# Sorting V as rows through DRAM in a Sinkhorn attention and feed-forward kernel

## The chip, the cores and the metric

The kernel runs on one core of a Trainium2 chip. The metric is the device time in microseconds (us) of one execution. The engines are TensorE (PE; its weight loads are shown as PEld), VectorE (DVE), ScalarE (ACT), GpSimd (POOL) and SyncE (SP). SP and POOL also issue DMAs; each has its own queue, and an engine takes its instructions in the order in which they are written.

## The reference

Four batches of eight heads, 768 positions, 64 elements a head. The 768 positions are cut into 8 blocks of 96. A small matrix P (8 x 8 for each batch and head) is made from `sort_net` by five rounds of softmax and column normalisation, and mixes the blocks of K and of V; attention then runs inside each block, and a feed-forward network with a squared ReLU follows.

```python
for _ in range(5):
    P = exp(P - P.max(-1)); P = P / (P.sum(-1) + 1e-9); P = P / (P.sum(-2) + 1e-9)
k_sorted = einsum('bhij,bhjcd->bhicd', P, k_b)      # the same for v
scores = scale * q_b @ k_sorted.T                   # block by block
attn = softmax(scores);  y = attn @ v_sorted
x = y as rows of 8 * 64 = 512                       # 3072 tokens
out = (s * relu(x @ w_in)**2 + b) @ w_out           # 512 -> 2048 -> 512
```

## The kernel before

The 3072 tokens are worked in eight tiles of 384 (two per batch: `half` 0 and 1, each of four blocks). For each tile `ffn1` multiplies by `w_in` (tiles `hps`, 128 matmuls of 384 columns), ACT takes the ReLU into `rt` and DVE squares it into `gt`; `ffn2` multiplies by `w_out` (tiles `ops`, three row groups of 16 matmuls of 512 columns), DVE adds scale and bias into `ot`, and SP stores it.

The order of the work is written out by hand. PE runs ffn1 of both tiles of a batch b, then ffn2 of both. `ffn2` takes a dictionary of slots: after each group of four `ops` matmuls the pieces in that slot are issued, and so the attention of the next batch n = b + 1 is laid into the two ffn2 of batch b. Slots 0 to 11 belong to one ffn2. In the first ffn2, slot 2 holds the three pieces of K sorting, slots 5 and 9 the four pieces of V sorting, slot 9 the first two score pieces, and slot 11 the first product with V:

```python
s0 = {2: [K(n, 0, "A"), K(n, 1, "D"), K(n, 2, "A")],
      5: [V(n, 0, "D"), V(n, 1, "A"), V(n, 2, "D")],
      9: [V(n, 3, "D"), SC(n, 0, 0), SC(n, 0, 1)],
      11: [P(n, 0, 0), SC(n, 0, 2), SC(n, 0, 3)]}
```

How K and V are sorted: `k_piece` (L252) takes 16 positions of K at a time. The 128 partitions hold head, block and half-block (`h j z`), and a matrix `PD[b]` made of P and masks (`build_pd`, from `jsel`, `bm`, `PT`, `RC`) picks and mixes. `v_piece` (L302) does the same for V with the roles of the operands changed: the data are the weights (128 x 64), so the result has the position on the partition, as `p_piece` needs it. For this V is first permuted from (c d) to (d c) into `VP`: for batch 0 by ACT during the start-up, for batches 1 to 3 by POOL in eight copies (`v_sort`, L171). A V piece is 32 matmuls of 64 columns and an evacuation of 1024 elements a partition from PSUM into `VS`; there are four pieces a batch. `VS` holds 48 positions on partitions 0 to 47 and 48 more on 64 to 111, with a column pair of ones (the softmax sum) behind each block's 64 values and zeros between; `fill_vs` writes these.

`s_piece` (tiles `sc`) makes the scores and ACT their exponentials `at`; `p_piece` (tiles `pv`, L352) multiplies by `VS`, and DVE divides into `x`. Queries are loaded as `qtok`, one DMA per block, and turned into `qt` by two DMA transposes on SP (`q_dma`, L294), which stand ahead of the first ffn2 of batch b; `x` is turned into `xt` by DMA transposes (`t_dma`, L389).

Loads for batch 1 are issued by POOL after the weights (`loads(1)`: K, V, eight of Q, then the eight permutes). Loads for batches 2 and 3 stand behind a small copy, `gate`, which waits for the first `gt` of a later ffn1. PSUM tiles come from two pools: `psa` (three buffers of two banks: `hps`, K, V, scores, pv) and `psb` (two of one bank: `ops` among others). `ot` has three buffers.

Of the kernel before, what the change touches and what calls it, by code (L numbers as in the profile page):

```python
# [9 lines left out]
FP = mybir.dt.float32  # L10
# [6 lines left out]
def spread(t, dims):  # L17

    return bass.AP(tensor=t.tensor, offset=t.offset, ap=[list(t.ap[0])] + dims)
# [3 lines left out]
def kernel(  # L23
# [32 lines left out]

    raw = [t.rearrange("b h (j z c) d -> b (h j z) (c d)", j=NB, z=2) for t in (q, k, v)]

    const = ctx.enter_context(tc.tile_pool(name="const", bufs=1))
    rawp = ctx.enter_context(tc.tile_pool(name="rawp", bufs=2))  # L60
    trp = ctx.enter_context(tc.tile_pool(name="trp", bufs=2))
# [5 lines left out]
    osb = ctx.enter_context(tc.tile_pool(name="osb", bufs=3))  # L67
    psa = ctx.enter_context(tc.tile_pool(name="psa", bufs=3, space=bass.MemoryType.PSUM))
    psb = ctx.enter_context(tc.tile_pool(name="psb", bufs=2, space=bass.MemoryType.PSUM))
    ctx.enter_context(tc.manual_schedule())  # L70


# [11 lines left out]
    def load(t, b, parts=1):  # L84
        ti = rawp.tile([128, C2, D], BF, tag=f"raw{t}", name=f"raw{t}")
        RAW[t, b] = ti
        n = C2 // parts
        for c in range(0, C2, n):
            nc.gpsimd.dma_start(out=ti[:, c:c + n, :].rearrange("p c d -> p (c d)"),
                                in_=raw["qkv".index(t)][b][:, c * D:(c + n) * D])  # L90

    QTOK = {}

    def load_q(b, ns=range(NB)):
# [4 lines left out]
        for n in ns:  # L99
# [2 lines left out]
    zeros = const.tile([128, 512], BF)  # L102
    nc.vector.memset(zeros[:, 0:128], 0.0)  # L103
    nc.vector.memset(zeros[:, 128:512], 0.0)  # L104
    VP = [const.tile([128, D, GAP], BF, name=f"vp{i}") for i in range(2)]
    KS = [const.tile([128, NG, 2, GAP], BF, name=f"ks{i}") for i in range(2)]
    VS = [const.tile([KR, 2 * NG, VW], BF, name=f"vs{i}") for i in range(2)]
    nc.vector.memset(VP[0][:, :, C2:GAP], 0.0)
    nc.vector.memset(KS[0][:, :, :, C2:GAP], 0.0)
    nc.vector.memset(sne[:, NB, :], 1e-9)  # L110

# [3 lines left out]
    idv = ident.rearrange("p (a e j z) -> p a e j z", a=NHP, e=2, j=NB)  # L115
    emat = const.tile([BH, B, 128], FP)
    nc.gpsimd.memset(emat, 0.0)
    nc.gpsimd.affine_select(out=emat, in_=emat, pattern=[[-H, B], [-1, H], [0, 2 * NB]], base=0,
                            channel_multiplier=1, compare_op=ALU.not_equal, fill=1.0)
    load("k", 0, 3)  # L120
    load_q(0, range(HB))
# [27 lines left out]
    def fill_vs(i):  # L149
        nc.gpsimd.memset(VS[i][:, :, D:VW], 1.0)  # L150
        nc.gpsimd.memset(VS[i][32:GAP, :, D:VW], 0.0)
        nc.gpsimd.memset(VS[i][32:C2, :, D:VW], 1.0)

    fill_vs(0)
    Z = []

    def warm(n, w=512):
# [4 lines left out]
                             start=True, stop=True)  # L162


    def permute(eng, b, src, cs=slice(0, C2), ds=slice(0, D)):
        o = VP[b % 2][:, ds, cs]
        i = src[:, cs, ds].rearrange("p c d -> p d c")
        if eng is nc.scalar:
            eng.copy(out=o, in_=i)
        else:  # L170
            eng.tensor_copy(out=o, in_=i)  # L171


    rstat = const.tile([BH, NB], FP)
    rrec = const.tile([BH, NB], FP)
    jsel = const.tile([128, NB], FP)
    bm = const.tile([128, 2 * 2 * NHP], FP)
    idle = [
        lambda: nc.vector.tensor_reduce(
            out=jsel, in_=ident.rearrange("p (h j z) -> p j h z", h=H, j=NB), axis=AX.XY, op=ALU.add),  # L180
# [8 lines left out]
    for it in range(5):  # L189
        nc.scalar.activation(out=sn, in_=sn, func=AF.Exp)  # L190
        if it >= 1:
            permute(nc.scalar, 0, v0f, slice((it - 1) * CV, it * CV))
# [26 lines left out]
    def take_p(b0, n, pe):  # L219

        bs = slice(b0, b0 + n)
        tmp = rtp.tile([128, n * NB, NB], FP, tag=f"tmp{n}", name="tmp")
        nc.vector.tensor_tensor(out=tmp, in0=pe.rearrange("p b i j -> p (b i) j"),
                                in1=spread(jsel, [[0, n * NB], list(jsel.ap[1])]), op=ALU.mult)
        nc.vector.tensor_reduce(out=PT[:, bs].rearrange("p b i -> p (b i)"), in_=tmp, axis=AX.X,
                                op=ALU.add)
        cs = rtp.tile([128, n], FP, tag=f"cs{n}", name="cs")
        nc.vector.tensor_reduce(out=cs, in_=PT[:, bs], axis=AX.X, op=ALU.add)
        nc.vector.reciprocal(out=RC[:, bs], in_=cs)

    def build_pd(b):
        pd = const.tile([128, 2, 2, NG], BF, name=f"pd{b}")
        nc.vector.scalar_tensor_tensor(
            out=pd.rearrange("p e z (a i) -> p (e z a) i", i=NB),
            in0=spread(bm, [list(bm.ap[1]), [0, NB]]), scalar=RC[:, b:b + 1],
            in1=spread(PT[:, b], [[0, 4 * NHP], list(PT.ap[2])]), op0=ALU.mult, op1=ALU.mult)
        PD[b] = pd
# [53 lines left out]
    def q_dma(b):  # L291
        qt = q_tile(b)
        for n0 in (0, HB):
            nc.sync.dma_start_transpose(  # L294
                out=qt[:, n0:n0 + HB].rearrange("p n a t -> p (n a) t"),
                in_=QTOK[b][:, n0:n0 + HB].rearrange("p n h d -> p (n h d)"))

    def v_piece(b, d0, eng):
        ps = psa.tile([128, CK, 2 * NG], FP, tag="a", name="tv")
        for d in range(CK):  # L300
            for z in range(2):
                nc.tensor.matmul(out=ps[z * GAP:(z + 1) * GAP, d, :],  # L302
                                 lhsT=VP[b % 2][:, d0 + d, :], rhs=PD[b][:, :, z, :],
                                 start=True, stop=True)
        evac(eng, VS[b % 2][:, :, d0:d0 + CK], ps[0:KR].rearrange("p d g -> p g d"))

# [150 lines left out]
        nc.sync.dma_start(out=out[r0:r0 + 128, ns], in_=ot[:, ns])  # L457


    take_p(0, 1, spread_p(0, 1))  # L460
    build_pd(0)

    nc.gpsimd.tensor_copy(out=ones[:, 0:1], in_=PD[0][:, 0, 0, 0:1])
# [31 lines left out]
    nc.gpsimd.memset(sel, 0.0)  # L495
    for r in range(0, 128, 32):
        nc.gpsimd.memset(sel[r:r + 1], 1.0)
    nc.gpsimd.memset(VP[1][:, :, C2:GAP], 0.0)
    nc.gpsimd.memset(KS[1][:, :, :, C2:GAP], 0.0)
    fill_vs(1)  # L500
    for t, src in ((s_bc, moe_s), (b_bc, moe_b)):
        nc.gpsimd.dma_start(out=t, in_=src.to_broadcast([128, 1]))

    def v_sort(b):
        for i in range(8):
            permute(nc.gpsimd, b, RAW["v", b], ds=slice(i * 8, (i + 1) * 8))

    def loads(b):
        load("k", b)
        load("v", b)  # L510
        load_q(b)
        v_sort(b)

    loads(1)

# [22 lines left out]
    def V(b, i, eng): return lambda: v_piece(b, i * CK, eng)  # L538
# [12 lines left out]
    ffn1(1, {-2: [TP(0, 1, 2, "D")], 1: [lambda: take_p(1, B - 1, PB), PDB(1)], 4: [PDB(2)],  # L551
             5: [PDB(3), sum_w], 7: [make_bias]}, ahead=3)
    gate = const.tile([128, 1], BF)

# [7 lines left out]
    for b in range(B):  # L562
        n = b + 1
        if b:
            ffn1(2 * b, {0: [gated_loads(n)]} if n < B else {})
            ffn1(2 * b + 1, {})
        if n == B:
            ffn2(2 * b, {})
            ffn2(2 * b + 1, {})
            break  # L570
        q_dma(n)
        s0 = {
            2: [K(n, 0, "A"), K(n, 1, "D"), K(n, 2, "A")],
            5: [V(n, 0, "D"), V(n, 1, "A"), V(n, 2, "D")],
            9: [V(n, 3, "D"), SC(n, 0, 0), SC(n, 0, 1)],
            11: [P(n, 0, 0), SC(n, 0, 2), SC(n, 0, 3)]}
# [35 lines left out]
```

## Time and profile before

| | us |
|---|---|
| median of 3 runs | 228.69 (228.53 to 228.84) |
| the profiled execution | 228.41 |
| its span, from first to last instruction | 226.6 |
| PE busy | 218.9 (97% of the span) |
| DVE busy | 124.5 |
| ACT busy | 99.5 |
| POOL busy | 68.2 |
| V pieces (L302) on PE, all four batches | 10.0 busy |
| permutes on POOL (L171), 24 of them | 19.0 busy |

The span is cut from one profiled execution; the difference to its own time lies before and after the recorded instructions. A line of a group gives the source line, the engine and operation, output and input tiles, the count, the busy time and the mean of one. A line of the chain in order of time gives the start in the span, the length and what it was. A matmul's busy time overlaps that of its neighbours, so lengths of PE work are best taken from the chain. A DMA's time to landing runs from its issue to its completion.

### The profile page before, as it was taken

To read this page: it belongs to the slowest core of one execution; us is meant where nothing else is said; L and a number is where in the kernel's file an instruction comes from. 1 tells how busy PE (TensorE), PEld (TensorE's weight loads), DVE (VectorE), ACT (ScalarE), POOL (GpSimd) and SP (SyncE) were. 2 spreads that over 40 slices of the span, in tenths; PEclk is the share of its full clock that TensorE was granted. 3 is DMA by queue.
4 is the path that set the end of the run, shared out by engine and by line. 5 is a ranking of instruction groups with operands and counts; after the bars stand their busy time and mean duration, and the time that the engine had idled before them with its cause. 6 is when DMAs were issued, how large, how long until landed. Compare 5 with 4: busy or idle time off the path is not lost.

```text
span 226.6 us, 5806 instructions
## 1 busy us (share of the span) xinstructions
PE 218.9 (97%) x2542; PEld 133.2 (59%) x2542; DVE 124.5 (55%) x223; ACT 99.5 (44%) x128; POOL 68.2 (30%) x112
## 2 busy tenths in 40 slices
PE   7996999999999999999999999999999999999993
PEld 8985656655555556665555556655566566654452
DVE  6766467553647634498656634498557543441121
ACT  4966476564325225637143236627152246550000
POOL 8467797338400009291000028490000000000000
PEclk9999999999999999999999999999999999999999
DMA  5999999999711558993112459991123240001212
GB/s 190 238 105 133 181 164 206 207 196 136 164 49 49 129 151 136 188 166 72 49 47 73 138 120 176 176 171 36 49 95 67 100 114 0 4 0 46 94 49 93
DMA packets 53930, 25.82 MB, mean 114 GB/s; under 512 B 44944, under 2 KB 49296, under 8 KB 53904
## 3 DMA queue, kind: packets, MB, share of 16 engines
q0 software_dynamic: 30864, 12.85, 47.1%
q1 hardware_dynamic: 23040, 12.59, 20.9%
q8 instruction: 20, 0.33, 0.6%
q14 instruction: 6, 0.05, 0.1%
HBM read 27.27 MB, written 6.29 MB: 148 GB/s over the span
## 4 chain that ended last, share of the span: by engine, by line
PE 86%; DVE 5%; DMA 3%; POOL 2%; ACT 1%; issue 1%; POOLq 0%
PE ops L433 36%; PE hps L408 36%; PE pv L352 3%; PE tv L302 3%; DMA qtok<-in_q_dram 3%; PE sc L317 2%; PE tp L252 2%; PE ops L446 2%; POOL wi L131 1%; DMA sne<-in_sort_net_dram 1%; ACT rt L422 1%; POOL qtok L100 1%; ACT sne L190 1%; PE scb L332 1%; DVE rstat L200 0%
## 5 line engine op out<-in xcount | busy, mean ns | idle before, releaser
L408 PE MATMUL hps<-xt,wi 128*128 128x384 bf16 x512 | 85.7, 326 | 0.3 <-DMA qtok<-in_q_dram 0.3
L433 PE MATMUL ops<-wo,gt 128*128 128x512 bf16 x368 | 85.7, 379 | 0.0
L422 ACT ACTIVATE rt<-hps 128x768 bf16<-128x768 f32 x64 | 51.1, 811 | 53.4 <-PE hps L408 45.6
L423 DVE TENSOR_TENSOR gt<-rt 128x768 bf16<-128x768 bf16 x64 | 46.9, 739 | 41.2 <-ACT rt L422 40.4
L408 PEld LDWEIGHTS <-wi 128*128 128x128 bf16 x512 | 49.3, 98 | 33.5 <-issue 0.6
L433 PEld LDWEIGHTS <-gt 128*128 128x128 bf16 x368 | 33.7, 98 | 36.9 <-issue 0.6
L454 DVE SCALAR_TENSOR_TENSOR ot<-ops,s_bc,bias 128x512 f32<-128x512 f32 (+1 forms) x25 | 18.2, 730 | 30.8 <-PE ops L433 28.2
L322 ACT ACTIVATE at<-sc 112x768 bf16<-112x768 f32 x28 | 21.3, 808 | 30.3 <-PE sc L317 30.3
L100 POOL DMA_DIRECT2D qtok<-in_q_dram x32 | 24.9, 793 | 18.4 <-DMA rawv<-in_v_dram 9.0
L360 DVE TENSOR_TENSOR x<-pv,rec 96x512 bf16<-96x512 f32 x32 | 22.0, 687 | 1.1
L243 DVE CAST vs<-tv 112x1024 bf16<-112x1024 f32 x11 | 13.2, 1222 | 10.8 <-PE tv L302 10.7
L171 POOL COPY vp<-rawv 128x384 bf16<-128x384 bf16 x24 | 19.0, 849 | 0.0
L558 POOL COPY gate<-gt 128x1 bf16<-128x1 bf16 x2 | 0.4, 193 | 56.6 <-DVE gt L423 56.6
L352 PEld LDWEIGHTS <-at 112*128 112x128 bf16 (+1 forms) x256 | 12.8, 101 | 7.2 <-ACT at L322 1.1
L352 PE MATMUL pv<-vs,at 112*128 112x66 bf16 (+1 forms) x256 | 13.9, 195 | 1.0 <-DVE vs L243 1.0
L161 PE MATMUL z<-zeros 128*128 128x140 bf16 (+1 forms) x132 | 11.7, 256 | 1.2 <-DVE zeros L104 1.2
L302 PEld LDWEIGHTS <-vp 128*64 128x64 bf16 x512 | 9.0, 113 | 3.9 <-issue 3.6
L161 PEld LDWEIGHTS <-zeros 128*128 128x128 bf16 x132 | 10.1, 111 | 1.4 <-DVE zeros L103 1.0
L302 PE MATMUL tv<-pd,vp 128*64 128x64 bf16 x512 | 10.0, 197 | 0.9 <-issue 0.8
L241 ACT CAST ks<-tp 128x1024 bf16<-128x1024 f32 x8 | 8.1, 1012 | 4.0 <-PE tp L252 3.9
L131 POOL DMA_DIRECT2D wi<-in_moe_w_in_dram x16 | 8.6, 552 | 2.6 <-DMA wi<-in_moe_w_in_dram 0.9
L241 ACT CAST vs<-tv 112x1024 bf16<-112x1024 f32 x5 | 5.1, 1019 | 9.3 <-PE tv L302 9.3
(76 smaller groups left out, 104.3 us busy)
## 6 DMA issues: line engine op xcount, KB each, us to landing
out_dram<-ot SPq DMA_DIRECT2D x23, 256.0 KB, 2.0
qtok<-in_q_dram POOLq DMA_DIRECT2D x32, 96.0 KB, 9.5
rawk<-in_k_dram POOLq DMA_DIRECT2D x3, 768.0 KB, 6.8
rawv<-in_v_dram POOLq DMA_DIRECT2D x3, 768.0 KB, 10.0
wi<-in_moe_w_in_dram POOLq DMA_DIRECT2D x16, 128.0 KB, 5.2
wo<-in_moe_w_out_dram POOLq DMA_DIRECT2D x4, 512.0 KB, 10.8
v0f<-in_v_dram SPq DMA_DIRECT2D x4, 384.0 KB, 4.3
rawk<-in_k_dram POOLq DMA_DIRECT2D x3, 256.0 KB, 7.9
```

The lines of the kernel that those rows point to most:

```text
L100: nc.gpsimd.dma_start(out=QTOK[b][:, n], in_=qv[:, n])
L161: nc.tensor.matmul(out=Z[0][:, 0:w], lhsT=zeros[:, 0:128], rhs=zeros[:, 0:w], start=True, stop=True)
L171: eng.tensor_copy(out=o, in_=i)
L302: nc.tensor.matmul(out=ps[z * GAP:(z + 1) * GAP, d, :], lhsT=VP[b % 2][:, d0 + d, :], rhs=PD[b][:, :, z, :], start=True, stop=True)
L322: nc.scalar.activation(out=at, in_=sc[0:KR, :, 0:TG], func=AF.Exp, scale=scale)
L352: nc.tensor.matmul(out=pv[0:m, e, n * VW:(n + 1) * VW], lhsT=atf[:, c0:c0 + m], rhs=VS[b % 2][:, e * NG + g0 + n, :], start=True, stop=True)
L360: nc.vector.tensor_tensor(out=x[:, :, hp * 128:(hp + 1) * 128].rearrange("p n (e d) -> p e n d", e=2), in0=pvv[:, :, :, 0:D], in1=rec.unsq ...
L408: nc.tensor.matmul(out=H1[i][:, f, 0:TG], lhsT=wi[:, hp, fc:fc + 128], rhs=xt[:, :, hp, :], start=(hp == 0), stop=(hp == NHP - 1))
L422: nc.scalar.activation(out=rt, in_=h, func=AF.Relu)
L423: nc.vector.tensor_tensor(out=gt[:, 2 * i:2 * i + 2, :], in0=rt, in1=rt, op=ALU.mult)
L433: nc.tensor.matmul(out=ops, lhsT=gt[:, f, m * 128:(m + 1) * 128], rhs=wo[:, f, :], start=(f == 0), stop=(f == NF - 1))
L454: nc.vector.scalar_tensor_tensor(out=ot[:, ns], in0=ops, scalar=s_bc, in1=BIAS[0][:, ns], op0=ALU.mult, op1=ALU.add)
```

## The change

Batch 0 is left as it was. For batches 1 to 3, K and V are loaded so that the partition order is (z, h, j): each half-block z has its own 64 partitions (`load_z`, two DMAs each, V ahead of K). V is no longer permuted. The new `v_rows` takes the block matrix `PV[b]` (64 x 64, once per z) as weights and V itself as the moving operand: four matmuls of 512 columns, one in each 64 x 64 tile of the array, sort 16 positions of each half-block. There are three such pieces a batch. The results have head and block on the partition; they are evacuated to `VO` and written by SP to a DRAM buffer `DV` laid out by position, two DMAs a piece, each of 1024 pieces of 128 bytes. `v_back` then reads `DV` back by position into `VS` with two DMAs on POOL. Before batch 1, `VS[1]` is filled with ones, copied into `DV` (which so gets the columns of ones), and its gap rows are set to zero.

```diff
+    def load_z(t, b):
+        ti = rawp.tile([128, C2, D], BF, tag=f"raw{t}", name=f"raw{t}")
+        RAW[t, b] = ti
+        for z in range(2):
+            nc.gpsimd.dma_start(out=ti[z * 64:(z + 1) * 64].rearrange("p c d -> p (c d)"),
+                                in_=rawz["qkv".index(t)][b, z])
...
+    DV = drp.tile([BLK, 2 * NG, VW], BF, name="dv")
+    VO = const.tile([128, 2, C2 // 2, D], BF)
...
-    nc.gpsimd.affine_select(out=emat, in_=emat, pattern=[[-H, B], [-1, H], [0, 2 * NB]], base=0,
+    nc.gpsimd.affine_select(out=emat[:, 0], in_=emat[:, 0], pattern=[[-1, H], [0, 2 * NB]], base=0,
...
+    for z in range(2):
+        em = emat[:, 1:B, z * 64:(z + 1) * 64]
+        nc.gpsimd.affine_select(out=em, in_=em, pattern=[[-H, B - 1], [-1, H], [0, NB]], base=-H,
...
+    def masks_z():
+        idz = ident.rearrange("p (z a e j) -> p z a e j", z=2, a=NHP, e=2)
...
+        PD[b] = build(b, bmz if b else bm, "pd").rearrange("p (e z a) i -> p e z (a i)", e=2, z=2)
+        if b:
+            PV[b] = build(b, bmv, "pv").rearrange("p m i -> p (m i)")
...
+    def v_rows(b, i, eng):
+
+        src, n = RAW["v", b], 8
+        ps = psa.tile([128, 2, n, D], FP, tag="a", name="vo")
+        for y in range(2):
+            for z in range(2):
+                zs, ys = slice(z * 64, (z + 1) * 64), slice(y * 64, (y + 1) * 64)
+                c0 = i * 2 * n + y
+                nc.tensor.matmul(out=ps[ys, z], lhsT=PV[b][zs], rhs=src[zs, c0:c0 + 2 * n - 1:2, :],
+                                 start=True, stop=True, tile_position=(z * 64, y * 64))
+        vo = VO[:, :, i * n:(i + 1) * n, :]
+        evac(eng, vo.rearrange("p z c d -> p z (c d)"), ps.rearrange("p z c d -> p z (c d)"))
+        dv = DV.rearrange("(z t c y) g w -> z t (y g) c w", z=2, y=2, c=n)
+        for z in range(2):
+            nc.sync.dma_start(out=dv[z, i, :, :, 0:D], in_=vo[:, z])
+
+    def v_back(b):
+
+        for z in range(2):
+            nc.gpsimd.dma_start(out=VS[b % 2][z * GAP:z * GAP + C2].rearrange("k g w -> k (g w)"),
+                                in_=DV[z * C2:(z + 1) * C2].rearrange("k g w -> k (g w)"))
...
-    nc.gpsimd.memset(VP[1][:, :, C2:GAP], 0.0)
     nc.gpsimd.memset(KS[1][:, :, :, C2:GAP], 0.0)
-    fill_vs(1)
+    nc.gpsimd.memset(VS[1], 1.0)
+    for z in range(2):
+        nc.sync.dma_start(out=DV[z * C2:(z + 1) * C2], in_=VS[1][z * GAP:z * GAP + C2])
+    nc.gpsimd.memset(VS[1][32:GAP], 0.0)
...
-    def v_sort(b):
-        for i in range(8):
-            permute(nc.gpsimd, b, RAW["v", b], ds=slice(i * 8, (i + 1) * 8))
-
     def loads(b):
-        load("k", b)
-        load("v", b)
+        load_z("v", b)
+        load_z("k", b)
         load_q(b)
-        v_sort(b)
...
-        q_dma(n)
+        if b:
+            q_dma(n)
         s0 = {
-            2: [K(n, 0, "A"), K(n, 1, "D"), K(n, 2, "A")],
-            5: [V(n, 0, "D"), V(n, 1, "A"), V(n, 2, "D")],
-            9: [V(n, 3, "D"), SC(n, 0, 0), SC(n, 0, 1)],
+            0: [V(n, 0, "D"), V(n, 1, "A"), V(n, 2, "D"), lambda: v_back(n)]
+               + ([] if b else [lambda: q_dma(n)]),
+            3: [K(n, 0, "A"), K(n, 1, "D"), K(n, 2, "A")],
+            9: [SC(n, 0, 0), SC(n, 0, 1)],
             11: [P(n, 0, 0), SC(n, 0, 2), SC(n, 0, 3)]}
```

In the changed kernel `V(n, i, eng)` calls `v_rows` instead of `v_piece`.

More of the change, by code (lines that the diff above doesn't have):

```diff
@@ L57 @@
     raw = [t.rearrange("b h (j z c) d -> b (h j z) (c d)", j=NB, z=2) for t in (q, k, v)]
+    rawz = [t.rearrange("b h (j z c) d -> b z (h j) (c d)", j=NB, z=2) for t in (q, k, v)]
     const = ctx.enter_context(tc.tile_pool(name="const", bufs=1))
@@ L69 @@
     psb = ctx.enter_context(tc.tile_pool(name="psb", bufs=2, space=bass.MemoryType.PSUM))
+    drp = ctx.enter_context(tc.tile_pool(name="drp", bufs=1, space=bass.MemoryType.DRAM))
     ctx.enter_context(tc.manual_schedule())
@@ L104 @@
     nc.vector.memset(zeros[:, 128:512], 0.0)
-    VP = [const.tile([128, D, GAP], BF, name=f"vp{i}") for i in range(2)]
+    VP = const.tile([128, D, GAP], BF)
     KS = [const.tile([128, NG, 2, GAP], BF, name=f"ks{i}") for i in range(2)]
     VS = [const.tile([KR, 2 * NG, VW], BF, name=f"vs{i}") for i in range(2)]
-    nc.vector.memset(VP[0][:, :, C2:GAP], 0.0)
+    DV = drp.tile([BLK, 2 * NG, VW], BF, name="dv")
+    VO = const.tile([128, 2, C2 // 2, D], BF)
+    nc.vector.memset(VP[:, :, C2:GAP], 0.0)
     nc.vector.memset(KS[0][:, :, :, C2:GAP], 0.0)
@@ L147, in load_w @@
             nc.gpsimd.dma_start(out=wo[:, fs, :], in_=wov[:, fs, :])
[L149 to L154, printed above, removed]
+    nc.gpsimd.memset(VS[0][:, :, D:VW], 1.0)
+    nc.gpsimd.memset(VS[0][32:GAP, :, D:VW], 0.0)
+    nc.gpsimd.memset(VS[0][32:C2, :, D:VW], 1.0)
+    for z in range(2):
+        em = emat[:, 1:B, z * 64:(z + 1) * 64]
+        nc.gpsimd.affine_select(out=em, in_=em, pattern=[[-H, B - 1], [-1, H], [0, NB]], base=-H,
+                                channel_multiplier=1, compare_op=ALU.not_equal, fill=1.0)
     Z = []
@@ L162, in warm, with permute @@
                              start=True, stop=True)
[L165 to L171, printed above, removed]
+    def permute(cs):
+        nc.scalar.copy(out=VP[:, :, cs], in_=v0f[:, cs, :].rearrange("p c d -> p d c"))
     rstat = const.tile([BH, NB], FP)
@@ L177 @@
     bm = const.tile([128, 2 * 2 * NHP], FP)
+    jselz = const.tile([128, NB], FP)
+    bmz = const.tile([128, 2 * 2 * NHP], FP)
+    bmv = const.tile([128, 2 * NHP], FP)
     idle = [
@@ L191 @@
         if it >= 1:
-            permute(nc.scalar, 0, v0f, slice((it - 1) * CV, it * CV))
+            permute(slice((it - 1) * CV, it * CV))
         if it in (1, 2):
@@ L217, in spread_p, with take_p @@
         return pe
-    def take_p(b0, n, pe):
+    def masks_z():
+        idz = ident.rearrange("p (z a e j) -> p z a e j", z=2, a=NHP, e=2)
+        nc.vector.tensor_reduce(
+            out=jselz, in_=ident.rearrange("p (z h j) -> p j z h", z=2, h=H), axis=AX.XY, op=ALU.add)
+        nc.vector.tensor_reduce(
+            out=bmz.rearrange("p (e z a) -> p e z a", e=2, z=2),
+            in_=idz.rearrange("p z a e j -> p e z a j"), axis=AX.X, op=ALU.add)
+        bv = bmz.rearrange("p (e z a) -> p e z a", e=2, z=2)
+        nc.vector.tensor_tensor(out=bmv.rearrange("p (e a) -> p e a", e=2), in0=bv[:, :, 0],
+                                in1=bv[:, :, 1], op=ALU.add)
+    def take_p(b0, n, pe, sel):
         bs = slice(b0, b0 + n)
@@ L223, in take_p @@
         nc.vector.tensor_tensor(out=tmp, in0=pe.rearrange("p b i j -> p (b i) j"),
-                                in1=spread(jsel, [[0, n * NB], list(jsel.ap[1])]), op=ALU.mult)
+                                in1=spread(sel, [[0, n * NB], list(sel.ap[1])]), op=ALU.mult)
         nc.vector.tensor_reduce(out=PT[:, bs].rearrange("p b i -> p (b i)"), in_=tmp, axis=AX.X,
@@ L229, in take_p, with build @@
         nc.vector.reciprocal(out=RC[:, bs], in_=cs)
-    def build_pd(b):
[L232 to L237, printed above, removed]
+    PV = {}
+    def build(b, m, name):
+        n = m.shape[1]
+        pd = const.tile([128, n, NB], BF, name=f"{name}{b}")
+        nc.vector.scalar_tensor_tensor(
+            out=pd, in0=spread(m, [list(m.ap[1]), [0, NB]]), scalar=RC[:, b:b + 1],
+            in1=spread(PT[:, b], [[0, n], list(PT.ap[2])]), op0=ALU.mult, op1=ALU.mult)
+        return pd
+    def build_pd(b):
+        PD[b] = build(b, bmz if b else bm, "pd").rearrange("p (e z a) i -> p e z (a i)", e=2, z=2)
+        if b:
+            PV[b] = build(b, bmv, "pv").rearrange("p m i -> p (m i)")
     def evac(eng, out, in_):
@@ L302, in v_piece @@
                 nc.tensor.matmul(out=ps[z * GAP:(z + 1) * GAP, d, :],
-                                 lhsT=VP[b % 2][:, d0 + d, :], rhs=PD[b][:, :, z, :],
+                                 lhsT=VP[:, d0 + d, :], rhs=PD[b][:, :, z, :],
                                  start=True, stop=True)
@@ L457, in store @@
         nc.sync.dma_start(out=out[r0:r0 + 128, ns], in_=ot[:, ns])
-    take_p(0, 1, spread_p(0, 1))
+    take_p(0, 1, spread_p(0, 1), jsel)
     build_pd(0)
@@ L537, in K, with V @@
     def K(b, i, eng): return lambda: k_piece(b, i * CK, eng)
-    def V(b, i, eng): return lambda: v_piece(b, i * CK, eng)
+    def V(b, i, eng): return lambda: v_rows(b, i, eng)
     def SC(b, h, i): return lambda: s_piece(b, h, i)
@@ L550 @@
              5: [SB(0, 1, 3), P(0, 1, 2)], 6: [TP(0, 1, 0, "D"), P(0, 1, 3)]}, ahead=3)
-    ffn1(1, {-2: [TP(0, 1, 2, "D")], 1: [lambda: take_p(1, B - 1, PB), PDB(1)], 4: [PDB(2)],
+    ffn1(1, {-2: [TP(0, 1, 2, "D")], 1: [masks_z, lambda: take_p(1, B - 1, PB, jselz), PDB(1)], 4: [PDB(2)],
              5: [PDB(3), sum_w], 7: [make_bias]}, ahead=3)
```

## The prediction

> **What bounds the kernel now.** I read the page first: the engine totals, then the chain that ended last.
>
> ```profile
> span 226.6 us, 5806 instructions
> PE 218.9 (97%) x2542; PEld 133.2 (59%) x2542; DVE 124.5 (55%) x223; ACT 99.5 (44%) x128; POOL 68.2 (30%) x112
> PE 86%; DVE 5%; DMA 3%; POOL 2%; ACT 1%; issue 1%; POOLq 0%
> ```
>
> PE is busy for 97% of the span and holds 86% of the chain; DVE, ACT and POOL have room. So work taken off PE after the start-up shortens the run, and any time for which PE waits lengthens it one for one. Next, the chain in order of time (start, us, what), at the first batch's ffn2, where batch 1 is prepared:
>
> ```profile
> 52.29 2.59 PE ops L433 x12
> 54.88 1.64 PE tp L252 x96
> 56.52 2.69 PE ops L433 x12
> 59.21 1.64 PE tv L302 x96
> 60.85 3.56 PE ops L433 x16
> 64.41 0.62 PE tv L302 x32
> 65.04 0.45 PE sc L317 x16
> 65.48 1.83 PE ops L433 x8
> 67.32 0.27 PE pv L352 x8
> ```
>
> PE runs on without a gap. Let T be the start of ffn2 (52.3 here, 102.3 and 152.3 for batches 2 and 3). V costs 1.64 + 0.62 = 2.26 us a batch, K 1.64, two score pieces 0.45, four ops matmuls 2.59/3 = 0.86. The first pv, which reads sorted V, stands at T + 15.0. Last, POOL before that stage, and DMA by stage:
>
> ```profile
> 30.99 0.90 POOL L497 MEMSET sel<- 1x128 f32 x4
> 31.95 0.96 POOL L498 MEMSET vp<- 128x1024 bf16 x1
> 32.84 0.96 POOL L499 MEMSET ks<- 128x1024 bf16 x1
> ...
> 35.60 0.57 POOL L89 DMA_DIRECT2D rawk<-in_k_dram  x1
> 36.13 0.58 POOL L89 DMA_DIRECT2D rawv<-in_v_dram  x1
> ```
>
> ```profile
> qtok<-in_q_dram POOLq DMA_DIRECT2D x32, 96.0 KB, 9.5
> qt<-qtok SPq DMA_TRANSPOSE x6, 3.8
> ```
>
> Batch 1's loads were issued from 35.6 and the last qtok at 52.1; the transposes of qt ran from 54.4, landing by 58.8: slack of about 6 us before sc at 65.0. For batch 2 the gate opened at 84.3, v landed at 95.4, q at 100.4: over 6 us before T.
>
> **What the Trainium skill says.** (1) "DMA: Bandwidth & Descriptors", Specifications: below 512 B a DMA does a read-modify-write and misses line rate. The trace has no small write to DRAM; its nearest row is qtok, 8 x 768 = 6144 packets of 128 B into SBUF, moved between about 94.7 and 100.3, so 5.6 us or 1100 packets/us. (2) The same page, Anatomy of one DMA: some 2 us fixed, mostly the receipt of the write, heaviest for HBM. The 256 KB stores agree: 2.0 us to landing with under 1 us of data. (3) "TensorEngine Tiling (Array Packing)", Tiling Modes: 64x64 gives four independent tiles. The trace has column tiles, cps (L527), 16 matmuls of 512 columns in 0.98 us, about four at once. (4) "TensorE: Matmul & The Clock Gate", Part 1: an idle window of 3.4 us halves PE's clock until a busy window passes. Here PE never idles so long and the clock reads 1.00; not shown.
>
> **The change part by part.**
>
> Removed on PE: 128 V matmuls a batch, 2.26 us. Added: 12 of 512 columns in four tiles; at the rate of cps (0.98/4 = 0.24 us for four) 0.72 us. Gain 1.54 us a batch, 4.6 in all. If the four went one after another (12 x 0.216 = 2.6 us by the ops rate), the gain would be a loss of 0.3; I take 0.72.
>
> Removed on POOL: 24 permutes, 19.0 us. Nothing on the chain waits for them: worth 0 by itself, but they let V move from slots 5 and 9 to slot 0. Evacuations: three of 1024 elements for four, 1.0 to 1.2 us each, on ACT and DVE, which are idle there: 0. Masks and the PV builds: about seven small DVE instructions at 0.2 to 0.35 us, 1.5 us, inside ffn1(1), where DVE waits for ACT most of the time: 0; without that cover at most 1.5. The split of emat's select and the order of the v and k loads: within POOL's 4.8 us of idle before ones, 0.
>
> Added to DMA, for each of batches 1 to 3: six SP issues of 1024 pieces, 6144 packets of 128 B into DRAM, then two POOL reads of 405 KB. The time W of the writes is the unknown that decides. Lower end: the qtok rate, 5.6 us. Upper: the transposes of qt, 2752 packets in 3.3 us, give 834/us and 7.4 us, and the read-modify-write could double that, 15 us. I take **W = 8.5 us**, half again the qtok row, as the pieces lie 132 B apart. A gain below 5.6 I leave to the rival.
>
> Timing in batches 2 and 3. V runs at slot 0, T + 0.9 to T + 1.2; DVE ends the last gt at T + 1.5 (L423, 0.56), the first evacuation at T + 2.7; SP issue 0.3 and DMA start 0.6 to 0.9: data from T + 3.6. Later pieces queue behind. End T + 3.6 + 8.5 = 12.1, receipt 1.5: T + 13.6. The read-back then starts: second issue 0.6, start 1.2 (rawk: issue 84.8, data from 86.0), last data 1.0 at 400 GB/s, landing 1.5 (rawv), together 4.3: **T + 17.9**. P(n,0,0) is due after 12 groups of ops, V, K and two score pieces: 10.4 + 0.7 + 1.6 + 0.45 = **T + 13.2**. PE waits 4.7. Behind it on PE everything queues, since it runs in order; ACT, DVE and the stores then wait for PE, with no further loss. On POOL the gate and the next loads queue behind the read-back's wait; the gate opens only some 30 us after T (84.3 for 52.3), so that costs 0. Net 4.7 - 1.5 = 3.2; the clock, after 4.7 us idle, costs nothing to 1.7 (half of a 3.4 window), I take 0.9. About +4 each, +8 for both. Stores behind the V writes on SP, and in batch 1 behind its wait for qtok, are late by some us, but three ot buffers at one per 3.5 us cover it.
>
> Batch 1 is worse, because POOL also gets two memsets of VS[1] with a wait between. Memsets cost about 0.82 ns an element (0.96 us for 1024, some 0.12 of it fixed): 4224 give 3.6 us each. POOL: ks from 32.0 to 32.9, first memset to 36.5; SP copies 405 KB to DRAM beside the wo loads, 4 to 6 us with the receipt, say to 41.7; second memset to 45.3; s_bc and b_bc 1.1. So rawv is issued at about 46.4 rather than 36.1 (the vp and small vs memsets, 1.6 us, are gone). What queues behind: v, k, q. By batch 2's times (issue to landing of the first 0.79 MB 6.8 us, of the second 10, end of q data 15.6) v lands at 53.2, k at 57, q data would end at 62. V is due at 53.2: wait 0 to 2, taken as 0.8. The V writes, from 56.5, now share the DMA engines with q: 5.6 + 8.5 = 14.1, to 70.6. The qt transposes, moved behind the V writes on SP and behind q's landing, take 4.4 (the 54.40 issue to 58.8): 75.0. SC(1,0,0) is due at T + 8.6 + 0.7 + 1.6 = 63.3: wait 11.7 (the 0.8 included). V is back by 70.6 + 5.8 = 76.4, ahead of P, 2.2 after SC. Net 11.7 - 1.5 + 1.7 (clock) = **+11.9**. With q and V overlapped without loss the wait could shrink to about 4.
>
> Sum: 11.9 + 8.1 = +20.0 on the profiled execution, 228.4 us (span 226.6 and 1.8 around it), 0.3 under the median 228.69: **248 us**.
>
> **The rivals.**
>
> A, likeliest, 0.58: the above, all three batches late, 241 to 259.
>
> B, 0.19: the 128 B writes into DRAM are much slower. At W = 15: batches 2 and 3 wait 11.2, net 11.4 each with the clock; batch 1's transposes land at 56.5 + 20.6 + 4.4 = 81.5, net +18.3; sum +41, 269. For: read-modify-write; pieces off alignment. Against: qtok's fast packets.
>
> C, 0.14: W = 5.6. Batches 2 and 3 wait 1.8, about +0.3 each; batch 1's transposes land at 72.1, +9. 238.
>
> D, the other side, 0.07: the DMA runs at several packets at once and the round trip hides. The place is P(n,0,0) at T + 13.2; it decides where W is below 3.8 us (1600 packets/us), and the gain survives if all waits together stay under 4.6 us. Then 228.4 - 4.6 = 223.8 with none, 227.5 with batch 1 still late by 3.7. Against it: no row shows such a rate. That the four tiles do not run together is a variant that adds 1.9 us to any case.
>
> Between C and D, 0.02: no change within 0.2% (0.46 us, about what a measurement of this kernel can tell).
>
> **How the numbers follow.** Slower in A, B and C: 0.91; same 0.02; faster 0.07. Range 231 to 272: it holds A and C with a part of their overlap with D's side, and B to just above its middle.
>
> **What would show it.** Right: PE idle ahead of pv (L406 or so, p_piece) ended by DMA vs<-dv in batches 2 and 3, about 4.7 us each; ahead of sc in batch 1, ended by the qt transposes, about 11; rawv issued near 46; granted clock under 1.00 just after the waits; V's PE time 0.7 a batch. Wrong: dv writes landing within 5 us of issue, or rawv issued before 40; a V stage over 2 us on PE; or waits in front of V itself, which would make the loads and not the round trip the bound.

## The result, and the profile after

The changed kernel takes 280.72 us (median of 6 runs, 277.95 to 281.57) against 228.68 us (6 runs), 1.2248 times as long (interval 1.219 to 1.2307). The profiled execution took 278.7 us, of which the span is 277.0, 50.4 us more than before. The forecast was 248 us in a range of 231 to 272: the direction was right, but a loss of 20 us was forecast and 52 was measured, above the upper end of the range.

The head of the page after, engine totals, granted clock in 40 slices, and shares of the chain:

```profile
span 277.0 us, 5160 instructions
PE 221.6 (80%) x2194; PEld 130.1 (47%) x2194; DVE 110.7 (40%) x226; ACT 99.9 (36%) x128; POOL 61.8 (22%) x100
PEclk9999999999557999999965899999985699999999
PE 53%; DMA 30%; POOL 8%; DVE 4%; issue 2%; SPq 1%; ACT 0%; POOLq 0%
```

PE's busy time is no lower, its share fell from 97% to 80%, and DMA, 3% of the chain before, now holds 30%. The clock dips three times, once a batch. PE's waits, in total (engine and line, what it waited for, us, times, longest):

```profile
PE pv L406 <- DMA vs<-dv: 32.7, 3, 14.8
PE sc L371 <- DMA qt<-qtok: 13.4, 1, 13.4
PE vo L338 <- DMA rawv<-in_v_dram: 1.5, 1, 1.5
PE tp L284 <- DMA rawk<-in_k_dram: 0.4, 1, 0.4
```

From the first ops after an ffn1 to the next ffn1, each batch took 29.2 us before; it now takes 50.5, 44.1 and 43.9, which is 50.9 more in all. The waits are 48.0 of it; V's shorter work on PE takes off 4.5, and the rest, some 7, is the slower clock after the waits. Batch 2 in the chain in order of time:

```profile
124.21 0.77 PE vo L338 x12
124.98 2.70 PE ops L487 x12
...
128.35 15.26 DMA dv<-VO
...
145.26 6.29 DMA vs<-dv
151.56 0.14 issue
151.69 0.62 PE pv L406 x8
152.32 0.76 PE sc L371 x16
153.07 1.82 PE ops L487 x4
```

The array tiles do what they should: V's 12 matmuls take 0.77 us where 128 took 2.26. But the last writes to DRAM land 15 us after they are issued, the read-back takes 6 more, and PE stands still. After it, sc takes 0.76 for 0.45, and four ops 1.82 for 0.86: the clock is at half. How the writes go shows in the DMA rate in 40 slices of the stretch 125 to 140 us, and in the times to landing:

```profile
GB/s 189 1 0 0 2 144 145 139 146 103 37 52 65 40 63 46 36 37 42 98 36 35 58 49 57 53 54 62 40 51 53 47 32 36 45 36 58 93 110 85
dv<-VO SPq DMA_DIRECT2D x18, 128.0 KB, 12.1
```

For some 1.5 us the writes move at the rate of qtok, 140 GB/s of 128 B pieces; then the rate falls to about 50 and stays there.

Batch 1, POOL's timeline and then PE's (in brackets the idle time ahead and what ended it):

```profile
33.30 3.62 POOL L553 MEMSET vs<- 112x4224 bf16 x1
43.07 3.61 POOL L556 MEMSET vs<- 32x4224 bf16 x1 [6.15 <-DMA dv<-vs]
...
47.73 1.12 POOL L99 DMA_DIRECT2D rawv<-in_v_dram  x2
```

```profile
79.02 0.83 PE L371 MATMUL sc<-qt,ks 64*128 64x96 bf16 x16 [13.37 <-DMA qt<-qtok]
79.78 3.58 PE L487 MATMUL ops<-wo,gt 128*128 128x512 bf16 x8
86.79 0.62 PE L406 MATMUL pv<-vs,at 112*128 112x66 bf16 x8 [3.44 <-DMA vs<-dv]
```

V's load is issued 11.6 us later than before (47.7 for 36.1), the qt transposes wait behind the V writes, and pv waits again after sc.

### The profile page after: what moved, and what is told of

It reads as the page before. It is cut to its first block, busy times and chain, and to the rows that moved or that the text cites. A ratio compares the mean times of both kernels' runs of the same rounds, so it can differ in the third digit from the quotient of the medians.

```text
span 277.0 us, 5160 instructions
## 1 busy us (share of the span) xinstructions
PE 221.6 (80%) x2194; PEld 130.1 (47%) x2194; DVE 110.7 (40%) x226; ACT 99.9 (36%) x128; POOL 61.8 (22%) x100
## 3 DMA queue, kind: packets, MB, share of 16 engines
q0 software_dynamic: 31344, 15.28, 43.9%
## 4 chain that ended last, share of the span: by engine, by line
PE 53%; DMA 30%; POOL 8%; DVE 4%; issue 2%; SPq 1%; ACT 0%; POOLq 0%
PE ops L487 23%; PE hps L462 23%; DMA dv<-VO 14%; DMA vs<-dv 7%; DMA rawk<-in_k_dram 3%; PE pv L406 3%; DMA qtok<-in_q_dram 3%; DMA dv<-vs 2%; POOL wi L144 2%; PE sc L371 2%; SPq L344 1%; POOL vs L556 1%; POOL vs L553 1%; PE tp L284 1%; PE ops L500 1%
## 5 line engine op out<-in xcount | busy, mean ns | idle before, releaser
L487 PE MATMUL ops<-wo,gt 128*128 128x512 bf16 x368 | 89.9, 393 | 0.0
L476 ACT ACTIVATE rt<-hps 128x768 bf16<-128x768 f32 x64 | 51.6, 811 | 48.5 <-PE hps L462 47.6
L477 DVE TENSOR_TENSOR gt<-rt 128x768 bf16<-128x768 bf16 x64 | 35.6, 558 | 47.0 <-ACT rt L476 46.7
L487 PEld LDWEIGHTS <-gt 128*128 128x128 bf16 x368 | 34.4, 100 | 40.2 <-issue 4.3
L376 ACT ACTIVATE at<-sc 112x768 bf16<-112x768 f32 x28 | 21.3, 808 | 84.1 <-PE sc L371 84.1
L406 PE MATMUL pv<-vs,at 112*128 112x66 bf16 (+1 forms) x256 | 14.9, 203 | 33.6 <-DMA vs<-dv 32.7
L406 PEld LDWEIGHTS <-at 112*128 112x128 bf16 (+1 forms) x256 | 13.7, 107 | 42.0 <-issue 36.1
L110 POOL DMA_DIRECT2D qtok<-in_q_dram x32 | 25.1, 816 | 11.1 <-DMA rawk<-in_k_dram 6.8
L413 DVE RECIPROCAL rec<-pv 96x8 f32<-96x8 f32 x32 | 6.4, 200 | 42.0 <-PE pv L406 42.0
L371 PE MATMUL sc<-qt,ks 64*128 64x96 bf16 x224 | 8.6, 224 | 13.5 <-DMA qt<-qtok 13.4
L349 POOL DMA_DIRECT2D vs<-dv x6 | 3.2, 532 | 72.4 <-DMA dv<-VO 46.4
L371 PEld LDWEIGHTS <-ks 64*128 64x128 bf16 x224 | 6.2, 104 | 15.5 <-issue 14.7
L273 ACT CAST ks<-tp 128x1024 bf16<-128x1024 f32 x8 | 8.1, 1012 | 10.1 <-PE tp L284 10.1
L609 POOL COPY gate<-gt 128x1 bf16<-128x1 bf16 x2 | 0.4, 188 | 50.4 <-DVE gt L477 50.4
L275 DVE CAST VO<-vo 128x1024 bf16<-128x1024 f32 x6 | 7.1, 1218 | 2.6 <-PE vo L338 2.6
## 6 DMA issues: line engine op xcount, KB each, us to landing
dv<-VO SPq DMA_DIRECT2D x18, 128.0 KB, 12.1
```

Source lines behind the costliest of these rows:

```text
L110: nc.gpsimd.dma_start(out=QTOK[b][:, n], in_=qv[:, n])
L371: nc.tensor.matmul(out=sc[:, e, n * BLK:(n + 1) * BLK], lhsT=KS[b % 2][pr, g0 + n].rearrange("p z c -> p (z c)"), rhs=QT[b][pr, half * HB ...
L376: nc.scalar.activation(out=at, in_=sc[0:KR, :, 0:TG], func=AF.Exp, scale=scale)
L406: nc.tensor.matmul(out=pv[0:m, e, n * VW:(n + 1) * VW], lhsT=atf[:, c0:c0 + m], rhs=VS[b % 2][:, e * NG + g0 + n, :], start=True, stop=True)
L476: nc.scalar.activation(out=rt, in_=h, func=AF.Relu)
L477: nc.vector.tensor_tensor(out=gt[:, 2 * i:2 * i + 2, :], in0=rt, in1=rt, op=ALU.mult)
```

## The experiments

Two theories stood after this. **The pitch**: the writes are slow because their 128 B pieces lie 132 B apart and so do not start on some boundary of the memory. **The size**: any 128 B write to DRAM is that slow. A third possibility was that the traffic beside them made them slow, and for batch 1 it was open how much the late loads cost and how much the writes.

### The writes by themselves: m_sizes and m_pitch

```diff
+    for i in range(6):      # first set of m_sizes, added after the last store
+        nc.sync.dma_start(out=at(i * 16 * 64 * 66, [[66, 128], [2 * 64 * 66, 8], [1, 64]]), in_=cut(i, 8))
...
```

> The kernel before, with eight sets of six SP transfers of 128 KB added after its last store, each set writing over the one before it and so waiting for it: (1) 6144 pieces of 128 B, 132 B apart, in the order of DV; (2) the same 128 B apart; (3) the same 256 B apart; (4) 128 B pieces 132 B apart, but the eight of one partition side by side and the partitions 1056 B apart; (5) 256 B pieces; (6) 512 B; (7) 1024 B; (8) a read of 6144 pieces of 128 B from DRAM into SBUF. Its time as a whole is of no interest. Theory 1 (the 132 B pitch is what is slow, since pieces share lines of the memory): set 1 takes about 15 us, sets 2 and 3 about 6 to 8, set 4 about 10. Theory 2 (any 128 B write to DRAM is slow, aligned or not): sets 1 to 4 all about 15, set 5 about 8, sets 6 and 7 about 3. Theory 3 (the writes were slow in the changed kernel only because of what ran beside them): set 1 about 6 us here. The read, set 8, is expected near the rate of qtok, 5.6 us, by all three.

Its sets ran into each other, so only some of it can be read. With nothing else running, set 1 again started at some 145 GB/s and fell to about 50 after 2 us, so traffic beside it was not the cause (theory 3 falls). Set 3 (128 B at 256 B) ran at 145 GB/s throughout, against the size theory. Set 4 (132 B apart in another order) began at that rate too, fell to about 40 GB/s, and landed up to 17.9 us after its issue. The read, set 8, moved its 0.79 MB at some 150 GB/s. Sets 2 and 5 started while the slow set ahead of each was still draining and prove nothing. m_pitch put them apart:

```diff
+    for i in range(5, -1, -1):   # every second set backwards: each waits for the one ahead
+        nc.sync.dma_start(out=at(i * 8 * 16384, [[64, 128], [1 * 16384 , 8], [1, 64]]), in_=cut(i, 8))
...
```

> The kernel before, with eight sets of six SP transfers of 128 KB from SBUF to DRAM after its last store; each set starts only when the one ahead of it has landed, and all have the same order (partitions side by side at the pitch given, the pieces of one partition 32 KB apart, 64 KB for the longer ones). In turn: (1) 128 B pieces at a pitch of 256 B; (2) 128 B at 128 B; (3) 128 B at 192 B; (4) 128 B at 160 B; (5) 256 B at 256 B; (6) 256 B at 260 B; (7) 128 B at 144 B; (8) 128 B at 132 B, the pitch of DV. Theory (pieces that do not start and end on a line of the memory are what is slow, their size is not): sets 1, 2, 3 and 5 take 6 to 8 us, set 8 and set 6 more than 12; sets 4 and 7 tell the size of the line (slow if it is 64 B; only set 7 slow if it is 32 B). Rival (neighbouring pieces under 256 B hold each other up, whatever their start): only sets 1 and 5 are fast, sets 2, 3, 4, 7 and 8 all take 12 or more.

SP's timeline of m_pitch, one line a set, in the order of the text above (start, us of issuing):

```profile
225.53 4.17 SPq L593 DMA_DIRECT2D scr<-wo  x6
232.51 4.10 SPq L595 DMA_DIRECT2D scr<-wo  x6
239.36 4.09 SPq L597 DMA_DIRECT2D scr<-wo  x6
246.26 4.08 SPq L599 DMA_DIRECT2D scr<-wo  x6
253.99 3.29 SPq L601 DMA_DIRECT2D scr<-wo  x6
259.01 3.28 SPq L603 DMA_DIRECT2D scr<-wo  x6
270.08 6.90 SPq L605 DMA_DIRECT2D scr<-wo  x6
283.58 8.81 SPq L607 DMA_DIRECT2D scr<-wo  x6
```

The distance from one start to the next is the time of a set with its landing: 128 B at a pitch of 256, 128, 192 and 160 B take 7.0, 6.9, 6.9 and 7.7 us; 256 B at 256 takes 5.0, and at 260 11.1; 128 B at 144 takes 13.5, at 132 about 16.5 (data until about 300). So it is where the pieces start and not their size or nearness: at pitches that are multiples of 32 B they are fast, at 144 B (a multiple of 16) and at 132 and 260 B (multiples of 4) they are slow. As 128 and 256 are themselves multiples of 32, start and end of a piece cannot be told apart here, and no run shows what happens inside a slow write. The pitch theory holds, and set 8 has the 16 us of the changed kernel.

### Taking the wait away, and the writes: e_nowait and e_nowrite

```diff
-        dv = DV.rearrange("(z t c y) g w -> z t (y g) c w", z=2, y=2, c=n)
+        dv = DW.rearrange("(z t c y) g w -> z t (y g) c w", z=2, y=2, c=n)   # e_nowait
```

> The changed kernel, but V's rows are written to a second DRAM buffer and the read-back reads the first, which holds ones: the writes stay, nothing waits for them on the way to pv, and sorted V is left out of the result for batches 1 to 3. If the wait of pv for the round trip is what batches 2 and 3 lose, their two ffn2 take 27.7 us each (29.2 before, less 1.5), against 44.1 and 43.9 in the changed kernel, and batch 1 keeps its wait for the qt transposes of about 13 us: about 243 us in all. If the writes also hold up stores and transposes so that PE waits for these, more than 250.

Measured: one run of 253.78 us (span 252.0). PE no longer waits before pv, but:

```profile
PE sc L372 <- DMA qt<-qtok: 16.5, 1, 16.5
PE sc L372 <- DVE x L415: 6.9, 2, 4.1
```

DVE itself waited 9.7 us for `DMA out_dram<-ot`: the stores stand behind the slow writes in SP's queue, no ot buffer comes free, and x, queued behind ot on DVE, is late; PE then waits for x 2.9 and 4.1 us, once in each of batches 2 and 3. So writes that nobody reads still cost some 7 us in batches 2 and 3, besides the wait for qt in batch 1. In the changed kernel DVE has no wait for stores: PE's longer wait for pv comes first.

```diff
-        for z in range(2):
-            nc.sync.dma_start(out=dv[z, i, :, :, 0:D], in_=vo[:, z])         # e_nowrite
```

> The changed kernel without the 18 writes of V's rows to DRAM; the read-back brings ones, so sorted V is left out for batches 1 to 3. What remains of the loss is the late start of batch 1's loads. Theory (the writes hold the ring ahead of the qt transposes): batch 1's wait before sc falls from 13.4 us to about 5, as q lands about 65 and the transposes take 4.4 after it; about 232 us in all. Rival (the late loads alone make batch 1's loss): the wait before sc stays at 10 or more, about 238.

Measured: one run of 234.90 us. PE's waits:

```profile
PE sc L369 <- DMA qt<-qtok: 3.6, 1, 3.6
PE vo L338 <- DMA rawv<-in_v_dram: 3.0, 2, 1.5
```

The wait before sc falls to 3.6 us, as the theory has it and against the rival's 10; the waits for V are why the total is 3 us above 232. Batches 2 and 3 went from ffn1 to ffn1 in 48.5 us each, where the kernel before has 50.0: the gain of 1.5 us a batch is there when the writes are left out. Batch 1 needs 39.2 us from ops to ffn1, 11.3 less than in the changed kernel and 10.0 more than before. So the late loads, with the clock falling after the waits, are about half of what batch 1 loses, and the writes the other half.

### The late loads: e_early

```diff
-    nc.gpsimd.memset(VS[1], 1.0)
-    for z in range(2):
-        nc.sync.dma_start(out=DV[z * C2:(z + 1) * C2], in_=VS[1][z * GAP:z * GAP + C2])
+    nc.vector.memset(VO[0:BLK], 1.0)      # DV is then filled from VO
```

> The changed kernel, with the ones of DV copied from VO, set by VectorE, so that POOL neither fills VS[1] with ones nor waits for a transfer before it clears the gap rows: batch 1's loads are issued about 9.6 us earlier. Theory (the qt transposes stand in SP's ring behind the slow writes of V): the writes still start near 56 and last 16 us, the transposes land near 76 in place of 79, gain about 3 us: 275 to 277 on the 278.7 us of the profiled execution. Rival (the late loads make the wait): gain about 9 to 10, 269.

Measured: one run of 276.32 us. The total lies where the first theory has it, but by luck: ffn2 began 4.6 us later than in the changed kernel, 2.6 of them VectorE's fill of VO, which stood on the start-up's path. From there batch 1 took 43.8 us in place of 50.5; sc waited 9.7 and V for nothing. The late loads were worth 6.8 us here, with the writes still slow, between the 3 and the 9 to 10 of the two theories.

### Other layouts: e_align, e_wide, e_best

```diff
-    DV = drp.tile([BLK, 2 * NG, VW], BF, name="dv")
+    DV = drp.tile([BLK, 2 * NG, D], BF, name="dv")          # e_align: rows of 64, ones stay in VS
```

> The changed kernel with DV 64 values wide, so that its 6144 pieces of 128 B stand side by side on multiples of 128 B; the ones stay in VS (DV is not filled with ones, POOL does not wait), and the read-back takes pieces of 128 B. Theory (the 132 B pitch makes the writes slow): the median dv write lands in about 4 us after issue instead of 12, and pv waits about 6 us in batches 2 and 3 instead of 14.7, since the read-back in pieces takes some 4 us longer; about 246 us in all. Rival (any 128 B write to DRAM is slow): the writes still land after 12 us, pv waits 16 or more, 275 or more.

Measured: one run of 263.43 us. Issues of e_align, KB each and median us to landing:

```profile
dv<-VO SPq DMA_DIRECT2D x18, 128.0 KB, 3.2
vs<-dv POOLq DMA_DIRECT2D x6, 384.0 KB, 10.7
```

The writes are fast, as the pitch theory says, but the total is 17 us above the 246 expected. The read-back, which now cuts whole rows of DRAM into 128 B pieces in SBUF, eats up the saving: it lands 10.7 us after issue (5.9 in the changed kernel, and I had allowed 4 more), and pv still waits up to 11.7.

```diff
+            nc.sync.dma_start(out=DV[:, :, c0:c0 + n, :].rearrange("g z c d -> g z (c d)"),
+                              in_=vo[y * 64:(y + 1) * 64].rearrange("p z c d -> p z (c d)"))   # e_wide
```

> The changed kernel with the layout turned round: V's rows are written to DRAM in 1024 B pieces by block (two SP transfers a sorting piece, 128 pieces each), and the read-back picks the positions out in 128 B pieces, six POOL transfers a batch; DV needs no ones and POOL does not wait for a transfer. If small writes at an odd pitch are the loss and small reads are not: writes land in about 2 us, the read-back in 5 to 6 us after them, pv waits 0 to 2 us in batches 2 and 3, batch 1 waits 2 to 4 us for the qt transposes: 226 to 233 us. If the round trip is slow in any layout (the receipts and the small pieces, on whichever side): pv waits 6 us or more, 245.

Measured: 255.75 us (4 runs), 1.1212 times before (1.112 to 1.1304). Neither number was met. pv waited 23.1 us over the three batches: a read lands 6.5 us after issue in the median, and the writes take 3.9, not the 2 expected (in batch 2 the first lands in 2.3, the last, issued while the first reads ran, in 6.6).

```diff
+            ffn1(2 * b + 1, {2: [V(n, 0, "D")], 4: [V(n, 1, "D")],
+                             6: [V(n, 2, "D"), lambda: v_back(n)]} if n < B else {})   # e_best
```

> As the turned-round layout, and in addition: the fills of KS[1] and VS[1] moved into POOL's idle stretch during the start-up, and V of batches 2 and 3 sorted in slots 2, 4 and 6 of the second ffn1 (in the PSUM buffers of ops, idle then), some 6 us ahead of ffn2. If the round trip is then hidden, PE keeps the 1.5 us a batch: 224 to 226 us, below the kernel before at 228.7. If the extra evacuations in ffn1 or batch 1's transposes hold PE up: 228 to 232.

An ffn1 has eight slots, one behind each eight of its matmuls: a tile takes 64 of them, and the 128 given further up are the two tiles of a batch. Measured: 256.58 us (4 runs), 1.1205 times (1.1127 to 1.1284), no better than e_wide and far from both figures. With the reads in flight earlier, the qt transposes became late (PE waited 10.3 us for them, 8.6 of it in batch 1) and pv still waited.

### The pitch alone, and the fill: e_pitch160, e_pad

```diff
-    VS = [const.tile([KR, 2 * NG, VW], BF, name=f"vs{i}") for i in range(2)]
+    VS = [const.tile([KR, 2 * NG, VR], BF, name=f"vs{i}") for i in range(2)]     # VR = 80; DV too
```

> The changed kernel with one size changed: rows of DV and VS are 80 values wide instead of 66, so the pitch of the 128 B pieces is 160 B, a multiple of 32 B, instead of 132 (VO takes the place of VP, which is free by then, to make room). Same number and size of pieces, same slots, same waits; the read-back still brings whole rows, a fifth longer. If the pitch is what made the writes slow: the median dv write lands in about 4 us instead of 12, the round trip is about 10 us shorter in each batch, pv waits about 4 to 5 us in batches 2 and 3 instead of 14.7; gain 25 to 30 us, about 250 us. If the number of small pieces makes them slow: no gain, about 282, as the fills of VS[1] get longer.

Measured: 261.42 us (4 runs), 1.1422 times before (1.1362 to 1.1482). Its issues and PE's waits:

```profile
dv<-VP SPq DMA_DIRECT2D x18, 128.0 KB, 4.6
```

```profile
PE pv L407 <- DMA vs<-dv: 17.0, 3, 6.2
PE vo L339 <- DMA rawv<-in_v_dram: 5.1, 2, 3.7
PE sc L372 <- DMA qt<-qtok: 3.7, 1, 3.7
```

One size changed, the same number of pieces: the writes land in 4.6 us instead of 12.1, the longest wait before pv falls from 14.8 to 6.2, sc's from 13.4 to 3.7, and the kernel gets 19 us faster (280.7 to 261.4), less than the 25 to 30 expected: the longer fill of VS[1] put off the loads (rawv issued at 50.0 instead of 47.7), and V waited 5.1 us for rawv.

```diff
-    nc.gpsimd.memset(VS[1], 1.0)
-    for z in range(2):
-        nc.sync.dma_start(out=DV[z * C2:(z + 1) * C2], in_=VS[1][z * GAP:z * GAP + C2])
+    nc.gpsimd.memset(VO[:, :, :, D:VR], 1.0)       # the ones travel with the pieces
```

> The 160 B pitch as before, and the columns of ones are written with the pieces (VO 80 values wide, pieces of 160 B), so that DV is not filled ahead and POOL does not wait for a transfer before batch 1's loads. This takes away the second thing held to make batch 1 late. Theory: rawv is issued near 40 instead of 50, V(1) waits for nothing, the wait before sc is 0 to 3 us, that before pv 4 to 6; batches 2 and 3 as with the pitch alone (about 6 us before pv); about 250 us against 261. If batch 1's lateness came from the transfers of V and q standing in each other's way and not from the late issue: 258 or more.

Measured: 252.91 us (4 runs), 1.1037 times before (1.099 to 1.1084). rawv is issued at 40.6, V waits for nothing, sc 1.4 us, as expected if the late issue was the cause; with transfers in each other's way it would have been 258 or more. pv waits 20.5 us over the three batches, 7.4 at most, more than the 4 to 6 expected: the round trip, now with fast writes, is still too long for the place it has.

### V sorted ahead of ffn2: e_hyb, e_hyb2

```diff
+            ffn1(2 * b + 1, {1: [V(n, 0, "D")], 3: [V(n, 1, "D")],
+                             5: [V(n, 2, "D"), lambda: v_back(n)]} if n < B else {})   # e_hyb
+        if n == 1:                      # batch 1 as before the change
+            s0[5] = [OV(n, 0, "D"), OV(n, 1, "A"), OV(n, 2, "D")]
```

> Batch 1 as in the kernel before (permuted by POOL, sorted in slots 5 and 9); batches 2 and 3 sorted as rows in four array tiles, in slots 1, 3 and 5 of the second ffn1 in the PSUM buffers of ops, written at a pitch of 160 B with the columns of ones in the pieces, read back as whole rows ahead of ffn2. If the round trip (about 7 us of writes, 6 us of read-back, from some 8 us ahead of ffn2) is over by the first pv, 12 us into ffn2, PE keeps 1.5 us in each of two batches: 225 to 226 us against 228.6. If the evacuations in ffn1, the qt transposes behind the writes or the longer rows cost as much, 228 or more.

This version fills the pads of VO while VP, whose place VO takes, holds batch 1's permuted V, so part of batch 1's V is ones; work and waits are whole. Measured: 238.76 us (6 runs), 1.0417 times (1.0368 to 1.0465). pv waited 5.8 us in two batches, the clock fell after each, and ffn2 began some 3 us later than before in the profiled execution.

```diff
+            ffn1(2 * b + 1, {0: [V(n, 0, "DA")], 2: [V(n, 1, "DA")],
+                             4: [V(n, 2, "DA"), lambda: v_back(n)]} if n < B else {})   # e_hyb2
+        if n > 1:                       # the first four pv pieces one slot later
+            s1[3] = s1[2]
+            s1[2], s1[1], s1[0] = s1[1], s1[0], [P(n, 0, 0)]
```

> The mixed version again (batch 1 as before the change; batches 2 and 3 sorted as rows ahead of ffn2 at a pitch of 160 B), with V in slots 0, 2 and 4 of the second ffn1, its evacuations split over VectorE and ScalarE, and the four pv pieces of the first half of batches 2 and 3 each one slot later: read-back some 2 us earlier, pv 1.3 us later, where the last version waited 2.6 and 3.1 us. The pads of VO are filled after batch 1's sorting. If the waits are then gone, PE keeps 1.5 us a batch in two batches: 225 to 227 us against 228.7. If a wait of over 2 us is left in each, 230 or more, and the kernel before stands.

Measured: 227.42 us (13 runs) against 229.3 (18 runs of before on the same chip), 0.9902 times (0.9868 to 0.9935): 19% faster than the changed kernel, and 1% faster than the kernel before, which is clear of the noise but small. Its waits:

```profile
PE ops L489 <- issue: 1.3, 8, 0.2
PE pv L408 <- DMA vs<-dv: 0.9, 1, 0.9
```

One wait of 0.9 us for the round trip is left. From ffn1 to ffn1 batch 2 took 50.0 us, as before the change, and batch 3 48.9, where e_nowrite shows 48.5 to be possible. So of the 1.5 us hoped for in each of two batches this profile shows 1.1, in one of them.

## Why the prediction was right or wrong

**Right: the bound, the sign and the places.** PE was the bound, V's work on it went from 2.26 to 0.77 us (0.72 forecast), and without the writes the gain was the 1.5 us a batch that I worked out. In batches 2 and 3 the round trip ended late, before pv, as case A said, and batch 1 lost most. In batch 2 (T = 123.35) the writes' data began at T + 3.7, where I had 3.6, and pv was due at T + 13.5, where I had 13.2.

**Wrong: W, the time of the writes.** This is the step that failed. I took 8.5 us, "half again the qtok row, as the pieces lie 132 B apart", or 10.0 with the landing; batch 2 took 16.6 (T + 3.7 to T + 20.3) and set 8 of m_pitch about 16.5. The qtok row has pieces of the same size, but neither their size nor writing to DRAM in place of reading from it was what counted. At the aligned pitches of 128, 160, 192 and 256 B the same number of pieces takes 6.9 to 7.7 us with the landing, so the qtok row itself, 5.6 without it, would have been about right there; the 4 B remainder more than doubled the time. I had named the alignment, but added only half of the row's time for it, where it was the main cost. Case B, with W = 15, had the writes right. It came to 269 for the 278.7 of the profiled execution because it shared the read-back with case A and had 3 us less for batch 1.

**Wrong: the read-back.** I had 4.3 us from the landing of the last write to data in VS; in batch 2 it was 7.9 (143.61 to 151.56). The second transfer was issued 1.65 us after that landing (0.6 forecast) and took 6.3. I had counted only the last transfer's data, at 400 GB/s; but the data of both, 0.81 MB, moved after 145.0, with next to nothing beside them, at some 180 GB/s. Why no faster stays open.

**Half right: batch 1.** The late issue was forecast at 46.4 and came at 47.7. The wait before sc was put at 11.7 with the wait for V in it; it was 13.4, with 1.5 before V and 0.4 before K. That V would then be back ahead of P was wrong: pv waited 3.4 more, a second stop with a second fall of the clock. Forecast net +11.9, measured 50.5 - 29.2 = 21.3.

**Mis-sized: the clock.** I took 0.9 us a wait in batches 2 and 3; the chain shows 0.31 on sc, 0.96 on ops and some 0.4 on the two pv, 1.7 in all, the upper value I gave. In batch 1 it fell twice: eight ops took 3.58 for 1.90, then sc, ops and pv lost time again as in batch 2.

**Wrong, though hidden: the stores.** That "three ot buffers at one per 3.5 us cover it" fails in e_nowait, where DVE waits 9.7 us for stores and PE 6.9 behind it.

By terms, batch 2: wait 14.8 (4.7 forecast), clock 1.7 (0.9), V -1.5, sum +15.0, against 44.1 - 29.2 = 14.9 measured. Of the 10.1 us by which the wait is longer, some 6.6 are the writes and some 3.6 the read-back. The two repairs give back 19 us for the pitch and 8.5 for the fill (280.7 to 261.4 to 252.9). Of the 24 that remain, 21.9 are waits, three before pv and one of 1.4 before sc; the rest is mostly the clock after them, less V's gain. That these need an earlier place is what e_hyb2 bears out, where pv waits 0.9 us in all.

**Small pieces, and when the clock falls.** "DMA: Bandwidth & Descriptors", Specifications, in the Trainium skill has the loss of rate begin below 512 B. The runs agree that 128 B pieces miss the rate of larger ones (6144 pieces of 128 B in 7 us, 3072 of 256 B in 5), but what more than doubled the time was where they start: 260 B pitch 11.1 us for 256 B pieces, 256 B pitch 5.0. "TensorE: Matmul & The Clock Gate", Part 1, has the clock halved after an idle window of about 3.4 us. The fall itself is borne out: granted clock 0.50 in the 2.4 us after batch 2's wait, 1.00 some 3 us after it ended. But the length of a wait alone does not tell whether it falls: after 2.6 us in e_hyb the clock read 0.51, after 2.9 us in e_nowait 1.00.

## What to carry to other kernels

Before small pieces are written to DRAM, work out the pitch in bytes: here 14 values of padding a row, which made it a multiple of 32 B, took 19 us off a kernel of 281. A round trip needs a place where its reader is due later than write, landing, read-back and the other transfers in the same queue together. Gaining 1.5 us of PE a batch is worth it only where that slack exists: inside ffn2 it did not, and with V sorted ahead of ffn2, a fast pitch and later pv pieces the whole gain was 1%. A fill that makes an in-order queue wait for a transfer delays everything behind it: the ones could travel with the pieces.

## What the runs showed that was not expected

- Misaligned writes run at full rate for the first 1.5 to 2 us (about 2000 pieces) and then at a third of it, alone (set 8 of m_pitch) or in the kernel; a test of fewer pieces would not have shown it.
- Writes that nobody waits for still held up stores and, through ot and the order of DVE, PE (6.9 us in e_nowait).
- The time of the start-up, until the first ffn2, differed by 2 us between kernels with the same start-up work (51.9 in the changed kernel, 53.9 in e_nowait); its cause stays open, and it blurs single runs by as much.
- The read-back of e_align, by POOL, took 10.7 us to landing and moved some 90 GB/s where nothing ran beside it (131 to 136 us); set 8 of m_sizes, by SP, wrote as many 128 B pieces into SBUF at the same 132 B pitch at some 150 GB/s. So that pitch in SBUF alone is not what makes it slow; queue and source layout differ too, and were not tried apart.
